# Two folded weight blocks come back from their exchange into other buffers

## The chip, the cores and the metric

The kernel runs on one core of a Trainium2 chip. The core has five engines that run side by side, each working through its own list of instructions in order: PE (TensorE, matrix products), DVE (VectorE), ACT (ScalarE), POOL (GpSimd) and SP (SyncE, which here only issues DMAs). ACT issues some DMAs too. The metric is the device time of one execution in microseconds (us); the time of a kernel is the median of its runs.

## The reference

Two attention branches A and B work on the same x (2048 rows of 448, in 16 heads of 28). Each branch has its own wqkv, w_phi and wo, and a gate mixes the two results:

```python
qkv = (x @ wqkv)                                  # per head q, k, v
pq = einsum("bhsd,hdf->bhsf", q, w_phi)           # the same w_phi for k
phi = concat([softmax(p), softmax(-p)], -1)       # for q and for k
kv = einsum("bhsf,bhsd->bhfd", phi_k, v);  z = sum_s phi_k
o = (phi_q @ kv) / (phi_q . z + 1e-6)
out = g * (o_A @ wo_A) + (1 - g) * (o_B @ wo_B)   # g = sigmoid(x . gate_w)
```

Since q is only ever used as q times w_phi, the kernel multiplies w_phi into the Q and K weights once ("the fold") and projects x with the folded weights. All is float32: each matrix is split into a high part (rounded for TensorE) and a low part (the rest), and products are summed over the parts.

## The kernel before, in words

The 2048 rows are cut into 16 tiles of 128, which are handled two at a time: eight steps u of branch A (loop from line 476), then eight steps of branch B (loop from line 580), then a tail whose order is a written list. A step of branch A or B has, on PE, a projection for K (`proj` with `wk`), one for V, one for Q where it is due, and `kv_acc`, which adds phi_k times V of the step before to the state. Around them: `k_shift` (DVE and POOL) takes the maximum off the K projection, `k_exp` (ACT) takes the exponentials, `k_sums` takes their sums (DVE, line 255), reciprocals (DVE, line 256) and products (POOL, line 264), and `kv_acc` (PE, line 289) waits for those products. `v_out` (ACT, line 272) copies a V projection out of PSUM. For Q: `q_front` (DVE, then DMAs `q_store` on SP and ACT to `qd` in DRAM), `q_load` (line 333, back from `qd` into `tq`), exponentials on ACT (341, 356), a POOL difference (349) and a DVE transposition (`q_turn`, 359); `num` (PE, 371) multiplies by the state. In branch B the A results are also finished: `a_turn` (DVE, 572), `n_rec` and `n_den`, `weights` (POOL, 403 and 404, with the gate), `n_mul` (POOL, 409).

Every engine works through its instructions in the order in which the program writes them, so a wait holds all that is written later for that engine. This holds for SP's DMAs too: a DMA whose source is not ready holds the ones behind it.

Branch B's folds go another way than A's. The strips of the weights are loaded (`load_strips`) and multiplied by w_phi on PE (`fold_strips`), and the products come out transposed. `turn_strips` turns 32x32 blocks on DVE (line 190), stores them to DRAM (`td`, four DMAs, line 192) and loads them back in the right layout (line 195 for three blocks of 128 rows, line 197 twice for the last 64 rows, which are held twice). `high_folded` (ACT, line 204) and `low_folded` (DVE, line 208) then make the high and the low part, each in one instruction of 128x1792. For K this begins in step u = 3 of branch A; the strips and the reloaded blocks lie in `wtb[1]`, the parts go to `wk[1]` (named wkb). For Q it begins in step u = 0 of branch B; strips and blocks lie in a tile named ctr, the parts go to `wq[1]` (named wka), which is first used by step u = 6 of branch B.

`wtb[0]` and `wtb[1]` are used for much else: the output weights come through them (`load_wo`, line 459; five of its seven loads are written in steps 4 and 5), and `q_turn` writes to them later. `wvr` holds the raw V weights: A's at the start, B's from step 0, read for the last time in step 3. `bd` and `wps` hold w_phi in two layouts; both have been read for the last time once the Q fold's products are through, and serve as output buffers in the tail.

Of the kernel before, what the change touches and what calls it, by code (L numbers as in the profile page):

```python
# [8 lines left out]
F32 = mybir.dt.float32  # L9
# [40 lines left out]
def hedgehog_mix(ctx: ExitStack, tc: tile.TileContext, xd, wv, wkt, wqt, wphi, wo, cmask, cpmask, out):  # L50
# [39 lines left out]
    make_identity(nc, ident)  # L90
    mask = raw.tile([PF, 4], F32, name="mask")
    wp = raw.tile([PF, 2, 4, HP], F32, name="wp")
    bd = wp_.tile([PF, 4, PF], F32, name="bd")
    wps = wp_.tile([P, D], F32, name="wps")
    wps = wps[:, :8 * HP].rearrange("p (b g m) -> p b g m", b=2, g=4)
    wk = [wp_.tile([P, 2, 4, D], F32R, name="wka"), wp_.tile([P, 2, 4, D], F32R, name="wkb")]
    wvs = [wp_.tile([P, 2, 4, DG], F32R, name="wva"), wp_.tile([P, 2, 4, D], F32R, name="wvb")]
    wq = [wp_.tile([P, 2, 4, D], F32R, name="wqa"), None]
# [23 lines left out]

    def load_wv(b, c, n=2, eng=nc.sync):
        w = (DG, D)[b]
        if c % 2 == 0:
            t = raw.tile([P, 2, w], F32, name=f"wvr{c}")
            for i in range(2):
                wvr[c + i] = t[:, i]
            if n == 2:
                return eng.dma_start(t, wv[c * P:(c + 2) * P, b * DG:b * DG + w].rearrange("(c p) n -> p c n", p=P))  # L130
        eng.dma_start(wvr[c], wv[c * P:(c + 1) * P, b * DG:b * DG + w])

    def high_w(wr, wh):
# [52 lines left out]
    def turn_strips(wt, ts, i):  # L186
        t = wt[:, :4 * D]
        o = t.rearrange("p (j i w m) -> p i w j m", i=2, w=2, m=HP)
        for j, ps in enumerate(ts):
            nc.vector.transpose(o[:, j], ps[:, :, :D].rearrange("p w (j m) -> p w j m", m=HP))  # L190
        for g in range(4):
            nc.sync.dma_start(td[i][:, g * P:g * P + P].rearrange("(j t) x -> t j x", t=HP),  # L192
                              t[HP * g:HP * g + HP].rearrange("t (j x) -> t j x", x=P))
        d = wt.rearrange("p (c x) -> p c x", c=4)
        nc.sync.dma_start(d[:, :3], td[i][:384].rearrange("(c p) x -> p c x", p=P))
        for p in (0, 64):
            nc.sync.dma_start(d[p:p + 64, 3], td[i][384:])

    def folded(wt, dst):
        return wt.rearrange("p (h m) -> p h m", m=HP)[:, :, :DH], [dst[:, i].rearrange("p c (h f) -> p (c h) f", f=DH) for i in range(2)]  # L200

    def high_folded(wt, dst):
        w, d = folded(wt, dst)
        nc.scalar.activation(d[0], w, AF.Copy)

    def low_folded(wt, dst, eng):
        w, d = folded(wt, dst)
        eng.tensor_tensor(d[1], w, d[0].bitcast(F32), OP.subtract)

    TERMS = [(c, 0, c) for c in range(3)] + [(4 + c, 0, c) for c in range(3)] + [(3, 0, 3)] + [(c, 1, c) for c in range(4)]  # L210

# [32 lines left out]
    def k_exp(k):  # L244
        for s in range(2):
            nc.scalar.activation(es[k][:, s], es[k][:, s], AF.Exp)  # L246
# [23 lines left out]
    def v_out(k, ps):  # L270
        v = vs[k % 2]
        nc.scalar.activation(v[:, :, :, :, :DH].rearrange("p w j q f -> p w (j q) f"), hb(ps[:, :, :D]), AF.Copy)  # L272
        if k < NU:
            nc.scalar.activation(glog[:, 2 * k:2 * k + 2], ps[:, :, D], AF.Copy)
# [65 lines left out]
    def q_exp0(k):  # L340
        nc.scalar.activation(eq[:, 0, :, :, :DH], tview(k), AF.Exp)
# [134 lines left out]
    for u in range(NU):  # L476

        if u in (2, 4):
            split_x(u // 2 + 1, 0, 4, 0)
        for c in WVS.get(u, ()):  # L480
            high_wv(1, c)
        if u == 5:
            nc.gpsimd.memset(eq[:, :, :, :, DH:], 0.0)
            for b in range(2):
                nc.gpsimd.memset(kvs[b], 0.0)
        if pq is not None:
            q_front(FRONTS[u - 1], pq)
            q_load(FRONTS[u - 1])
            pq = None
        pk = proj(u, wk[0], two_tile())  # L490
        if u > 1:
            k_sums(u - 1)
        if u in (2, 4):
            split_x(u // 2 + 1, 0, 4, 1)
        k_shift(u, pk)
        if u == 1:
            fold(wtqa, wq[0])
            k_sums(0)
        if u == 2:
            pq = proj(0, wq[0], two_tile())  # L500
            kv_acc(0)
        if u > 1:
            pv = proj(u, wvs[0], two_tile())
            v_out(u, pv)
        k_exp(u)

        if u == 0:
            wtqa = load_wt(wtb[0], wqt[0])
            load_x(2, 0, 4)
            for c in range(0, 4, 2):  # L510
                load_wv(1, c)
        if u == 1:
            load_strips(wtb[1], wkt[1])
            for r in range(4):
                nc.sync.dma_start(wps[HP * r:HP * r + DH], wphi[DH * r:DH * r + DH])
            nc.sync.dma_start(wos.rearrange("g (a f) n -> g a (f n)", f=DH),
                              wo.rearrange("(a g f) n -> g a (f n)", g=4, f=DH))
        if u in (2, 4):
            split_x(u // 2 + 1, 0, 4, 2)
        for c in WVS.get(u, ()):  # L520
            low_wv(1, c, nc.gpsimd)
        for c in WOS.get(u, ()):
            high_wo(c)
            low_wo(c)
        if u == 2:
            load_wo(0, 1)
            load_x(3, 0, 4)
        if u == 4:
            high_folded(wtb[1], wk[1])
            low_folded(wtb[1], wk[1], nc.vector)  # L530
            load_wo(4, 5, 2, 3)
        if u == 5:
            load_wo(6)
            start.close()
            mid = ctx.enter_context(tc.tile_pool(name="mid", bufs=1, side="right"))
            wtqb = load_strips(mid.tile([P, 2048], F32, name="ctr"), wqt[1])
        if u > 1:
            kv_acc(u - 1)
        if u == 3:
            turn_strips(wtb[1], fold_strips(1, wtb[1]), 0)  # L540
        if u == 7:
            pf = fold_strips(1, wtqb)
        if u == 5:
            pq = proj(FRONTS[u], wq[0], two_tile())
        if u == 6:
            q_exp0(0)
            q_min(0)
            q_exp1(0)
        if u == 7:
            q_turn(0)  # L550
# [29 lines left out]
    for u in range(NU):  # L580
# [5 lines left out]
        if n >= 0:  # L586
            a_turn(n)
            n_rec(n)
        q_exp0(m)
        q_min(m)  # L590
        if u == 0:
            turn_strips(wtqb, pf, 1)
# [11 lines left out]
        if u == 0:  # L604
            kv_acc(k - 1)
            state_copy(0)
            high_folded(wtqb, wq[1])
        else:
            k_sums(k - 1)
            if u == 1:  # L610
                n_mul(n)
        k_shift(k, pk)
        if u == 0:
            state_turn(0)
            q_turn(m)
            low_folded(wtqb, wq[1], nc.vector)
        pv = proj(u, wvs[1], two_tile())
        v_out(k, pv)
        k_exp(k)
        if u > 0:  # L620
            q_turn(m)
        if u == NU - 1:
            woh, wol = [wp_.tile([P, 7, D], F32R, name=n) for n in ("wkb", "wvb")]
            for w, d in ((woh, wod[0]), (wol, wod[1])):
                nc.sync.dma_start(w.bitcast(F32), d)
# [10 lines left out]

    obs = [wp_.tile([P, D], F32, name=n) for n in ("bd", "wps")]
    osb = wp_.tile([P, 2, 8, 8, DH], F32, name="wqa")  # L640
    qps, reads, maxs, mns, hls = {}, {}, {}, {}, {}
    A, B, C = (turn[0] + 2) % 3, turn[0], (turn[0] + 1) % 3
# [254 lines left out]
```

## Time and profile before

| | before |
|---|---|
| time, median of 3 runs | 361.88 us (359.70 to 362.72) |
| profiled execution, its own time | 361.31 us |
| profiled execution, span | 359.5 us |
| PE busy | 343.5 us (96%) |
| DVE busy | 275.1 us (77%) |
| POOL busy | 261.9 us (73%) |
| ACT busy | 121.4 us (34%) |
| mean granted clock of TensorE | 0.984 |

Times inside the profile are counted from the first instruction. Of the span, 1.8 us less than the execution's own time, almost all is PE work; what is left is where PE waits. Step u of branch A ends with its `kv_acc`: step 4's lies at 69 us in the profile for the products of step 3, step 5's at 87 us for those of step 4. Branch B begins at 115 us with a Q projection, its step 1 at 134 us, its step 2 at 150 us.

### The profile page before, as it was taken

What the parts mean: (1) busy time and instruction counts of PE and PEld (TensorE: products, weight loads), DVE (VectorE), ACT (ScalarE), POOL (GpSimd) and SP (SyncE); (2) the same over time, 40 slices, a digit from 0 to 9 for tenths busy, and PEclk for the clock granted to TensorE, in tenths of its full rate; (3) what the DMA queues carried; (4) which work ended last, traced back from release to release, by engine and by line L of the source; (5) the groups of instructions that cost most, each with busy time, mean ns of one, the idle gap of its engine ahead of it and who ended that gap; (6) DMA issues with size and microseconds to landing.
All of it is one profiled execution on the core that took longest, in us unless ns stands there. A gap on an engine that the chain in (4) does not pass through costs nothing.

```text
span 359.5 us, 8502 instructions
## 1 busy us (share of the span) xinstructions
PE 343.5 (96%) x3599; PEld 301.2 (84%) x3599; DVE 275.1 (77%) x315; ACT 121.4 (34%) x170; POOL 261.9 (73%) x228
## 2 busy tenths in 40 slices
PE   8999999983999979999999999999999999999995
PEld 7999888872988869898988989898888978888894
DVE  4328765526478779979989898899899999989740
ACT  4525335141244242133142231313223364434331
POOL 2453799745469423898988878886779999999850
PEclk9999999995899999999999999999999999999999
DMA  8796246751673761333313222349573472664111
GB/s 233 228 327 143 102 110 169 223 168 54 218 152 107 133 190 21 92 102 104 104 53 104 82 85 93 107 127 366 155 231 98 131 189 71 175 185 128 53 52 51
DMA packets 38958, 49.58 MB, mean 138 GB/s; under 512 B 11784, under 2 KB 32104, under 8 KB 38632
## 3 DMA queue, kind: packets, MB, share of 16 engines
q1 hardware_dynamic: 33768, 44.90, 42.5%
q10 hardware_dynamic: 5152, 4.13, 3.8%
q8 instruction: 28, 0.46, 0.6%
q14 instruction: 10, 0.08, 0.1%
HBM read 29.27 MB, written 21.36 MB: 141 GB/s over the span
## 4 chain that ended last, share of the span: by engine, by line
PE 72%; DMA 8%; POOL 7%; DVE 7%; ACT 2%; issue 1%; SPq 1%; POOLq 0%; ACTq 0%; DVEq 0%
PE two L225 45%; PE out L826 16%; PE two L371 4%; PE kv L289 3%; POOL e L264 3%; DMA wtb<-wos 2%; PE two L154 2%; DMA ctr<-td 2%; DMA wtb<-td 1%; DMA xrb<-in_xt 1%; DMA td<-wtb 1%; DVE sm L255 1%; POOL wva L409 1%; SPq L192 1%; PE kv L371 1%
## 5 line engine op out<-in xcount | busy, mean ns | idle before, releaser
L264 POOL TENSOR_TENSOR e<-e,rs 128x896 f32<-128x896 f32 x32 | 53.8, 1703 | 28.4 <-DVE rs L256 28.4
L225 PE MATMUL two<-wka,xg 128*128 128x448 f32 x352 | 73.8, 366 | 0.0
L225 PEld LDWEIGHTS two<-wka,xg 128*128 128x128 f32 x352 | 65.2, 188 | 6.3 <-issue 0.8
L272 ACT ACTIVATE vs<-two 128x896 f32<-128x896 f32 x16 | 14.7, 918 | 84.4 <-PE two L225 84.4
L225 PE MATMUL two<-wqa,xg 128*128 128x448 f32 x176 | 39.3, 380 | 2.1 <-ACT vs L272 2.1
L225 PEld LDWEIGHTS two<-wqa,xg 128*128 128x128 f32 x176 | 33.7, 195 | 6.5 <-ACT vs L272 2.6
L225 PE MATMUL two<-wva,xg 128*128 128x450 f32 x176 | 38.9, 372 | 0.2 <-ACT wva L134 0.2
L246 ACT ACTIVATE e<-e 128x896 f32<-128x896 f32 x32 | 28.7, 946 | 27.9 <-POOL e L242 27.8
L225 PE MATMUL two<-wvb,xg 128*128 128x448 f32 x176 | 37.2, 366 | 0.0
L359 DVE STREAM_TRANSPOSE wtb<-xrb 128x2048 f32<-128x2048 f32 x16 | 36.6, 2288 | 0.0
L225 PE MATMUL two<-wkb,xg 128*128 128x448 f32 x176 | 36.6, 363 | 0.0
L225 PEld LDWEIGHTS two<-wva,xg 128*128 128x128 f32 x176 | 33.1, 189 | 3.7 <-ACT wva L134 0.7
L255 DVE TENSOR_REDUCE sm<-e 128x32 f32<-128x896 f32 x32 | 33.0, 1072 | 4.2 <-ACT e L246 4.2
L242 POOL TENSOR_TENSOR e<-mx,e 128x896 f32<-128x896 f32 x16 | 27.2, 1703 | 11.6 <-DVE mx L241 11.5
L225 PEld LDWEIGHTS two<-wvb,xg 128*128 128x128 f32 x176 | 33.0, 188 | 2.8
L225 PEld LDWEIGHTS two<-wkb,xg 128*128 128x128 f32 x176 | 33.0, 188 | 2.3
L826 PE MATMUL out<-wkb,e 128*128 128x448 f32 x154 | 34.7, 370 | 0.1
L826 PEld LDWEIGHTS out<-wkb,e 128*128 128x128 f32 x154 | 28.6, 188 | 4.0 <-issue 0.8
L349 POOL TENSOR_TENSOR xrb<-qmn,tq 128x896 f32<-128x896 f32 x16 | 28.2, 1760 | 3.5 <-issue 3.1
L316 DVE TENSOR_REDUCE qmx<-two 128x32 f32<-128x896 f32 x14 | 15.0, 1073 | 16.0 <-PE two L225 16.0
L409 POOL TENSOR_TENSOR wva<-wva,cdd 128x896 f32<-128x896 f32 (+1 forms) x12 | 26.5, 2210 | 0.8
L409 POOL TENSOR_TENSOR ctr<-ctr,cdd 128x896 f32<-128x896 f32 (+1 forms) x12 | 26.6, 2213 | 0.6
(113 smaller groups left out, 579.9 us busy)
## 6 DMA issues: line engine op xcount, KB each, us to landing
tq<-qd SPq DMA_DIRECT2D x16, 448.0 KB
qd<-uq ACTq DMA_DIRECT2D x32, 112.0 KB
qd<-uq SPq DMA_DIRECT2D x32, 112.0 KB
od<-wva SPq DMA_DIRECT2D x8, 448.0 KB
wqa<-od SPq DMA_DIRECT2D x8, 448.0 KB
wod<-wtb SPq DMA_DIRECT2D x14, 224.0 KB
xrb<-in_xt SPq DMA_DIRECT2D x2, 1024.0 KB
out<-bd SPq DMA_DIRECT2D x8, 224.0 KB
```

The source lines that it names most:

```text
L225: nc.tensor.matmul(ps[:, i, :n], x[:, xc, o:o + P], w[:, k, wc], start=j == 0, stop=j == 10)
L242: nc.gpsimd.tensor_tensor(e5[:, 1], mx[:, 1, :, :, None].to_broadcast([P, 2, H, DH]), e5[:, 0], OP.subtract)
L246: nc.scalar.activation(es[k][:, s], es[k][:, s], AF.Exp)
L255: nc.vector.tensor_reduce(sm[:, s], e[:, s].rearrange("p (h f) -> p h f", f=DH), AX.X, OP.add)
L264: nc.gpsimd.tensor_tensor(e3, e3, rs[:, s, :, None].to_broadcast([P, HA, DH]), OP.mult)
L272: nc.scalar.activation(v[:, :, :, :, :DH].rearrange("p w j q f -> p w (j q) f"), hb(ps[:, :, :D]), AF.Copy)
L316: nc.vector.tensor_reduce(mx, p4, AX.X, OP.max)
L349: nc.gpsimd.tensor_tensor(eq[:, 1, :, :, :DH], mn.rearrange("p c a -> p a c")[:, :, :, None].to_broadcast([P, 8, 4, DH]), tview(k), OP.sub ...
L359: nc.vector.transpose(wtb[k % 2], eq.rearrange("p s a c f -> p (s a c f)"))
L371: nc.tensor.matmul(banks[r][32 * g:32 * g + 32, 256 * s:256 * s + 256], kvt[b][32 * r:32 * r + 32, s, g], eT[32 * r:32 * r + 32, s, g], st ...
L409: nc.gpsimd.tensor_tensor(c3, c3, dd.to_broadcast([P, 8, hi - lo, DH]), OP.mult)
L826: nc.tensor.matmul(outs[t % 2][:, :D], (hi, lo)[x][:, c], w[:, c], start=x == 0 and n == 0 and c == 0, stop=x == 1 and c == 6)
```

## The change

The blocks of the K fold come back into `wvr`, now one tile of 128x2048, instead of `wtb[1]`, in five DMAs instead of three: one per block of 128 rows, two for the last block. The high part is made by four ACT instructions of 128x448, written ahead of `k_exp` of step 4 and no longer behind it; the low part by four on DVE.

The blocks of the Q fold come back two at a time into `bd` and `wps`, which are made 512 wide. Their loads are written behind the V projection, `v_out` and `k_exp` of step u = 0 of branch B; they were written ahead of the Q store of that step. The high parts of the first two blocks follow there on ACT, their low parts on POOL; the other two blocks are loaded into the same two tiles when those have been read, their high parts are made by ACT in step 1 and their low parts by DVE in step 2.

```diff
-    bd = wp_.tile([PF, 4, PF], F32, name="bd")
-    wps = wp_.tile([P, D], F32, name="wps")
-    wps = wps[:, :8 * HP].rearrange("p (b g m) -> p b g m", b=2, g=4)
+    bd = wp_.tile([P, 512], F32, name="bd")[:PF, :4 * PF].rearrange("p (g c) -> p g c", g=4)
+    wps = wp_.tile([P, 512], F32, name="wps")[:, :8 * HP].rearrange("p (b g m) -> p b g m", b=2, g=4)
+    wvrs = raw.tile([P, 2048], F32, name="wvr")
...
     def load_wv(b, c, n=2, eng=nc.sync):
         w = (DG, D)[b]
-        if c % 2 == 0:
-            t = raw.tile([P, 2, w], F32, name=f"wvr{c}")
-            for i in range(2):
-                wvr[c + i] = t[:, i]
-            if n == 2:
-                return eng.dma_start(t, wv[c * P:(c + 2) * P, b * DG:b * DG + w].rearrange("(c p) n -> p c n", p=P))
+        t = wvrs[:, c // 2 * 2 * DG:][:, :2 * w].rearrange("p (c n) -> p c n", c=2)
+        wvr[c] = t[:, c % 2]
+        if n == 2:
+            wvr[c + 1] = t[:, 1]
+            return eng.dma_start(t, wv[c * P:(c + 2) * P, b * DG:b * DG + w].rearrange("(c p) n -> p c n", p=P))
...
-        d = wt.rearrange("p (c x) -> p c x", c=4)
-        nc.sync.dma_start(d[:, :3], td[i][:384].rearrange("(c p) x -> p c x", p=P))
-        for p in (0, 64):
-            nc.sync.dma_start(d[p:p + 64, 3], td[i][384:])
...
+    def load_folded(i, bufs, cs):
+        for c in cs:
+            for p in (0, 64)[:1 + (c == 3)]:
+                n = P if c < 3 else 64
+                nc.sync.dma_start(bufs[c][p:p + n], td[i][c * P:c * P + n])
+
+    def high_folded(bufs, dst, cs):
+        for c in cs:
+            nc.scalar.activation(dst[:, 0, c].rearrange("p (h f) -> p h f", f=DH),
+                                 bufs[c].rearrange("p (h m) -> p h m", m=HP)[:, :, :DH], AF.Copy)
+
+    def low_folded(bufs, dst, cs, eng):
+        for c in cs:
+            h, l = [dst[:, i, c].rearrange("p (h f) -> p h f", f=DH) for i in range(2)]
+            eng.tensor_tensor(l, bufs[c].rearrange("p (h m) -> p h m", m=HP)[:, :, :DH], h.bitcast(F32), OP.subtract)
...
+        if u == 4:
+            high_folded(fk, wk[1], range(4))
         k_exp(u)
...
         if u == 4:
-            high_folded(wtb[1], wk[1])
-            low_folded(wtb[1], wk[1], nc.vector)
+            low_folded(fk, wk[1], range(4), nc.vector)
             load_wo(4, 5, 2, 3)
...
             turn_strips(wtb[1], fold_strips(1, wtb[1]), 0)
+            fk = [wvrs[:, 512 * c:512 * c + 512] for c in range(4)]
+            load_folded(0, fk, range(4))
...
         q_exp0(m)
+        if u == 1:
+            high_folded(fq, wq[1], (2, 3))
         q_min(m)
...
             state_copy(0)
-            high_folded(wtqb, wq[1])
...
             q_turn(m)
-            low_folded(wtqb, wq[1], nc.vector)
         pv = proj(u, wvs[1], two_tile())
         v_out(k, pv)
         k_exp(k)
-        if u > 0:
+        if u == 0:
+            fq = [wp_.tile([P, 512], F32, name=n) for n in ("bd", "wps")] * 2
+            for cs in ((0, 1), (2, 3)):
+                load_folded(1, fq, cs)
+                if cs[0] == 0:
+                    high_folded(fq, wq[1], cs)
+                    low_folded(fq, wq[1], cs, nc.gpsimd)
+        else:
             q_turn(m)
+        if u == 2:
+            low_folded(fq, wq[1], (2, 3), nc.vector)
```

What this does to the order of the instructions shows at three places. The first is ACT around the K fold, steps 4 and 5 of branch A; before it reads (272 is `v_out`, 246 is `k_exp`, 204 is `high_folded`):

```order
L272 ACTIVATE vs_150<-two_748 128x32x28
L274 ACTIVATE glog<-two_748 128x2
L246 ACTIVATE e<-e 128x896 x2
L204 ACTIVATE wkb<-wtb_124 128x1792
L272 ACTIVATE vs_151<-two_853 128x32x28
L274 ACTIVATE glog<-two_853 128x2
```

and now, with `high_folded` in line 202:

```order
L272 ACTIVATE vs_151<-two_747 128x32x28
L274 ACTIVATE glog<-two_747 128x2
L202 ACTIVATE wkb<-wvr 128x448 x4
L246 ACTIVATE e<-e 128x896 x2
L272 ACTIVATE vs_152<-two_858 128x32x28
L274 ACTIVATE glog<-two_858 128x2
```

The one large copy has become four, and they have moved past the exponentials of step 4. The second place is SP's queue around the Q fold, before (192 stores to `td`, 195 and 197 load it back, 325 and 333 are the Q store and load, 566 and 568 take the gate through DRAM):

```order
L192 DMA td_88<-ctr 32x14x128 x4
L195 DMA ctr<-td_88 128x3x512
L197 DMA ctr<-td_88 64x512 x2
L325 DMA qd_92<-uq_129 32x4x224 x2
L333 DMA tq_131<-qd_92 128x896
L566 DMA gd<-glog 32x4x16 x4
L568 DMA gate<-gd 128x64
L325 DMA qd_93<-uq_130 32x4x224 x2
L333 DMA tq_132<-qd_93 128x896
```

and now (the loads are in line 198, the gate in 569 and 571):

```order
L191 DMA td_88<-ctr 32x14x128 x4
L325 DMA qd_92<-uq_129 32x4x224 x2
L333 DMA tq_131<-qd_92 128x896
L198 DMA bd<-td_88 128x512
L198 DMA wps<-td_88 128x512
L198 DMA bd<-td_88 128x512
L198 DMA wps<-td_88 64x512 x2
L569 DMA gd<-glog 32x4x16 x4
L571 DMA gate<-gd 128x64
L325 DMA qd_93<-uq_130 32x4x224 x2
L333 DMA tq_132<-qd_93 128x896
```

The Q store and load now stand ahead of the reloads of the fold, and the second pair of reloads, which waits until `bd` and `wps` have been read, stands ahead of the gate. The third place is ACT around the Q fold, before (294 copies the state, 562 is the gate's exponential):

```order
L294 ACTIVATE kvs_75<-kv 128x8x28
L204 ACTIVATE wka<-ctr 128x1792
L272 ACTIVATE vs_150<-two_1312 128x32x28
L246 ACTIVATE e<-e 128x896 x2
L562 ACTIVATE glog<-glog 128x16
L341 ACTIVATE xrb<-tq_131 128x32x28
L356 ACTIVATE xrb<-xrb 128x32x28
```

and now (the gate's exponential is in line 565):

```order
L294 ACTIVATE kvs_75<-kv 128x8x28
L272 ACTIVATE vs_151<-two_1312 128x32x28
L246 ACTIVATE e<-e 128x896 x2
L202 ACTIVATE wka<-bd 128x448
L202 ACTIVATE wka<-wps 128x448
L565 ACTIVATE glog<-glog 128x16
L341 ACTIVATE xrb<-tq_131 128x32x28
L202 ACTIVATE wka<-bd 128x448
L202 ACTIVATE wka<-wps 128x448
L356 ACTIVATE xrb<-xrb 128x32x28
```

`v_out` and `k_exp` of branch B's first step now come ahead of the fold's high parts, and the gate's exponential stands behind the first two of them.

More of the change, by code (lines that the diff above doesn't have):

```diff
@@ L193, in turn_strips @@
                               t[HP * g:HP * g + HP].rearrange("t (j x) -> t j x", x=P))
-        d = wt.rearrange("p (c x) -> p c x", c=4)
-        nc.sync.dma_start(d[:, :3], td[i][:384].rearrange("(c p) x -> p c x", p=P))
-        for p in (0, 64):
[L197 to L208, printed above, removed]
+    def load_folded(i, bufs, cs):
[11 more added lines that the diff above has]
+            eng.tensor_tensor(l, bufs[c].rearrange("p (h m) -> p h m", m=HP)[:, :, :DH], h.bitcast(F32), OP.subtract)
     TERMS = [(c, 0, c) for c in range(3)] + [(4 + c, 0, c) for c in range(3)] + [(3, 0, 3)] + [(c, 1, c) for c in range(4)]
@@ L635, in hedgehog_mix @@
             kv_acc(k - 1)
-    obs = [wp_.tile([P, D], F32, name=n) for n in ("bd", "wps")]
+    obs = [wp_.tile([P, 512], F32, name=n)[:, :D] for n in ("bd", "wps")]
     osb = wp_.tile([P, 2, 8, 8, DH], F32, name="wqa")
```

## The prediction

> **What bounds the kernel now.** I read the page's summary first: the busy time of PE, and its slices of busy time and granted clock.
>
> ```profile
> PE 343.5 (96%) x3599; PEld 301.2 (84%) x3599; DVE 275.1 (77%) x315; ACT 121.4 (34%) x170; POOL 261.9 (73%) x228
> PE   8999999983999979999999999999999999999995
> PEclk9999999995899999999999999999999999999999
> ```
>
> PE is busy nearly everywhere. A slice is 9 us, and two places show a dent: the ninth and tenth slices (near 80 us), where the clock falls too, and the fifteenth (near 130 us). These are the two folds of branch B. Next the chain of waits around the first dent, in order of time (start, duration, what):
>
> ```profile
> 66.77 4.16 DMA td<-wtb
> ...
> 70.97 0.38 SPq L195
> ...
> 71.45 0.51 SPq L197
> ...
> 72.05 4.96 DMA wtb<-td
> ...
> 77.12 1.71 ACT wkb L204
> ...
> 78.86 2.03 DVE wkb L208
> 80.88 2.00 DVE sm L255 x2
> ...
> 82.90 0.56 DVE rs L256
> ...
> 83.60 3.36 POOL e L264 x2
> ...
> 87.01 1.72 PE kv L289 x64
> ```
>
> The K fold goes out to DRAM and comes back at 77.0; ACT makes the whole high part, DVE the whole low part, and only then does DVE come to the sums of step 4, which PE needs through POOL. The timeline shows what PE loses, and that the exponentials had long been done:
>
> ```profile
> 71.70 1.79 ACT L246 ACTIVATE e<-e 128x896 f32<-128x896 f32 x2 [1.35 <-POOL e L242]
> 74.64 4.68 PE L225 MATMUL two<-wva,xg 128*128 128x450 f32 x22
> 87.01 1.72 PE L289 MATMUL kv<-e,vs 128*29 128x56 f32 x64 [7.68 <-POOL e L264]
> 88.66 6.16 PE L225 MATMUL two<-wqa,xg 128*128 128x448 f32 x22
> ```
>
> PE stands 7.68 us. The projection after it takes 6.16 us, against 4.68 in the row above, since the clock has fallen. The windows of one us (PE busy, then four engines, granted clock, DMA share, GB/s) say when:
>
> ```profile
> 75.00:76.00 1.00, 0.94 (x4) 1.00 1.03 279
> 76.00:77.00 1.00, 0.03 (x1) 1.00 0.31 82
> ...
> 81.00:82.00 1.00, 0.00 (x0) 0.00 (x0) 1.00 (x2) 0.00 (x0) 0.00 (x0) 0.75 0.03 8
> 91.00:92.00 1.00, 1.00 (x5) 0.88 (x5) 0.00 (x0) 1.00 (x3) 1.00 (x1) 0.63 0.21 77
> ```
>
> (The first two are of POOL alone: busy, clock, DMA share, GB/s.) The clock halves at about 81.5, 2.2 us after PE went idle at 79.3, and is whole again at about 91.7, so 4.7 us of work run at half speed and cost 2.35 us. Last, the timeline around the second dent:
>
> ```profile
> 121.53 1.16 DVE L318 TENSOR_TENSOR uq<-two,qmx 128x448 f32<-128x448 f32 x2
> 125.61 4.74 PE L225 MATMUL two<-wvb,xg 128*128 128x448 f32 x22
> 126.01 1.05 SPq L325 DMA_DIRECT2D qd<-uq  x2
> 131.41 1.70 ACT L204 ACTIVATE wka<-ctr 128x1792 fp32r<-128x1792 f32 x1 [5.30 <-DMA ctr<-td]
> 131.96 0.34 SPq L333 DMA_DIRECT2D tq<-qd  x1
> 133.01 0.90 ACT L272 ACTIVATE vs<-two 128x896 f32<-128x896 f32 x1
> 133.96 4.76 PE L225 MATMUL two<-wqa,xg 128*128 128x448 f32 x22 [2.08 <-ACT vs L272]
> 135.49 0.20 ACT L562 ACTIVATE glog<-glog 128x16 f32<-128x16 f32 x1
> 136.26 1.73 SPq L566 DMA_DIRECT2D gd<-glog  x4
> 140.70 0.34 SPq L568 DMA_DIRECT2D gate<-gd  x1
> ```
>
> ACT waits for the Q fold until 131.4, with `v_out` behind it; PE needs that copy and stands 2.08 us. The fold itself is not due until step 6. After this PE hardly waits, but POOL is close behind it:
>
> ```profile
> 139.09 0.35 POOL L388 TENSOR_TENSOR cdd<-wva,crs 128x64 f32<-128x64 f32 x1 [8.75 <-DVE crs L383]
> 142.74 0.27 POOL L403 TENSOR_TENSOR cden<-cden,gate 128x32 f32<-128x32 f32 x1 [0.89 <-DMA gate<-gd]
> 145.05 3.36 POOL L264 TENSOR_TENSOR e<-e,rs 128x896 f32<-128x896 f32 x2 [1.64 <-DVE rs L256]
> 161.61 3.36 POOL L264 TENSOR_TENSOR e<-e,rs 128x896 f32<-128x896 f32 x2
> 165.02 0.84 PEld L289 LDWEIGHTS kv<-e,vs 128*29 128x29 f32 x64 [0.58 <-POOL e L264]
> ```
>
> From 145.05 POOL works without a gap until its products of 161.61, and PE's state update at 165.02 waits 0.58 us for them. So what PE wins at 132 counts only as far as POOL's 145.05 moves too.
>
> **The change, part by part.** The profiled execution took 361.31 us with a span of 359.5; I sum against 361.31, which is 0.57 below the median of the three runs (361.88) and well inside their range of 3 us.
>
> *K's reload.* The stores to `td` and the start of the reload at 70.97 stay. `wvr` was read for the last time in step 3, so the target costs no wait. Five DMAs take the place of three: with 0.48 us from one issue to the next in the rows above, the last goes out at about 73.0 and no longer at 72.05. I let it land at 77.1 all the same: the DMA engines were full (share 1.03) until 76, so bytes and not issues set the end. Were it the issue, it would be 78.0; were it the last byte, 76.3.
>
> [...] The row of the four stores to `td`, which land 4.16 us after the last of them was issued, is of overlapped DMAs, and I keep the overlap.
>
> *K's high and low parts.* I need the price of one block of 128x448 on ACT and on POOL:
>
> ```profile
> 106.61 0.56 ACT L134 ACTIVATE wtb<-wtb 128x448 fp32r<-128x448 f32 x1
> 107.24 1.16 POOL L137 TENSOR_TENSOR wtb<-wtb 128x448 fp32r<-128x448 f32 x1 [2.37 <-ACT wtb L134]
> ```
>
> Three blocks are done while the fourth lands. The last costs ACT 0.56; DVE's last low part (a quarter of 2.03, some 0.55) runs beside the exponentials. These now come behind: `k_exp` waits for the fold and ends at 77.2 + 0.56 + 1.79 = 79.5 and no longer at 73.5. That costs `v_out` of step 5 nothing, since PE ends its V projection at 79.3. DVE's first sum needs only the first half, done at 78.65. So from the landing to the sums: 0.1 + 0.56 + 0.9 = 1.6 us and no longer 80.88 - 77.01 = 3.9. The second half is ready at 79.5, before the first sum ends (78.7 + 1.0). The rest of the chain (2.00, 0.56, 3.36) is unchanged. Gain 3.9 - 1.6 - 0.1 for the landing = **2.2 us**; with the other landings 1.3 and 3.0. PE still stands some 5.5 us, and the clock falls as before, so I leave those 2.35 us in.
>
> *Output weights.* SP no longer waits for `low_folded` with the loads of blocks 2 and 3; they come earlier, behind the reload in the same queue. Nothing waited for them before, nor will now: no gain.
>
> *Q's ACT wait.* `v_out` no longer stands behind the fold: it starts when PE's V projection is through (130.4) and ends at 131.3; the stall of **2.08 us** goes. `k_exp`, with its 1.79 us, ends at 133.1. What is late next is POOL's 145.05, which hangs on two things. One is DVE, which in order must first do the gate's arithmetic after ACT's exponential, then `a_turn`, the Q work and the sums. ACT's exponential comes behind two high parts: 133.1 + 2 x 0.56 = 134.3 against 135.49, if the first two blocks have landed by 133. I expect that: SP's Q store, whose data DVE has ready at 122.7, goes out 3.2 us earlier than 126.01, without the fold's megabyte ahead of it. A pair like this is seen later:
>
> ```profile
> 142.36 0.79 SPq L325 DMA_DIRECT2D qd<-uq  x2
> 145.54 0.34 SPq L333 DMA_DIRECT2D tq<-qd  x1
> ```
>
> With 3.2 us from store to load, and a us more since the `td` stores are still moving, the Q load goes out at 127, the two blocks behind it at 127.5 and 128, and they land by 132 even with 4 us each. So DVE comes 1.2 us earlier.
>
> *Q's low parts and the gate.* POOL makes two low parts, 2 x 1.16 us, from 133.8 to 136.1, in its idle 8.75 us: free. But SP's second pair of loads waits for each of them, and behind it stand the gate's DMAs, the Q store of step 1 and its load. SP issues the second pair at 134.9 and 136.1 to 137.2 (three issues, 0.48 apart), then the gate's four stores at 137.3 against 136.26. With 4.4 us to the gate's load (136.26 to 140.70) and 2.0 more until POOL starts (142.74), POOL's line 403 starts at 143.7, 1.0 late. POOL then needs 0.7 us to its products: 144.5 against 145.05. DVE would have allowed 143.9. So POOL gains 0.55; I take **0.4**, since the ACT queue's Q store now falls on the gate's load. The bounds are 1.2 (the gate not late) and a loss of 3.8 (worked out in the last rival).
>
> *Q's other parts.* The second pair's high parts, 1.1 us, stand on ACT ahead of the exponential of line 356, which waits for POOL anyway; their low parts cost DVE 1.1 us in step 2, where it has lost the 2.03 of line 208 for good. I cost both at nothing; uncovered it would be 1.1 us. The wider tiles and the single V tile move no instruction.
>
> Sum: 361.31 - 2.2 - 0.4 = **358.7 us**. From 165 on PE is the bound and both terms reach the end.
>
> **The rivals.** *The clock does not fall.* PE's idle stretch shrinks from 7.7 to 5.5 us. If that no longer halves the clock, the 2.35 us go too: 358.7 - 2.35 = 356.4. Against it: here the clock fell 2.2 us into the idle time. [...] Chance 0.10.
>
> *The gate is not late.* The low parts or the loads go faster, and DVE alone decides: 361.31 - 2.2 - 1.2 = 357.9. For it: there is 1 us only between the two. Chance 0.14.
>
> *The split brings nothing for K.* Five smaller DMAs end by their issues or later (78.0 to 78.6), and the gain falls to about 1: 361.31 - 1.0 - 0.4 = 359.9. For it: the reload's last 128 KB took 4.96 us from issue to landing before. Against: the full engines. [...] Chance 0.16.
>
> *SP's new waits decide, and it gets slower.* If the first two blocks land as late as before's fold did after its last issue (4.96 us), behind a Q load that still goes out at 131.96, they land at 137.5. ACT's high parts end at 138.7, POOL's low parts at 140.5, SP's gate stores go out at 141.7, the gate lands 6.4 us later, and POOL's products start at 148.9 and no longer at 145.05: a loss of 3.8 and, with K's gain, 361.31 + 3.8 - 2.2 = 362.9. It decides from a landing at about 136 on (a loss of 2.2). For it: two waits in a row on one queue. Against: 4 us between that and the landing that I expect. Chance 0.08.
>
> **How the numbers follow.** The forecast has what is left, 0.52, with 358.7 and its own range 357.7 to 359.9: K's landing 1 us either way, less the extremes. The runs before spread over 3 us, so a median may lie 1 us off. The range leaves out most of the last rival and half of the first: 356.5 to 361.2. A measurement of this kernel tells about 1% from no change; 1% below 361.88 is 358.3, above it 365.5. Below 358.3: most of the first two rivals and a quarter of the forecast, 0.36. Above 365.5: a part of the last rival and a little for what I do not see, 0.05. Within: 0.59.
>
> **What would show it.** Right: line 202's last copy of K ends at 77.7 or so, DVE's sums of step 4 start 2 us earlier and PE's stall near 80 us is about 5.5; the stall of 2.08 is gone, DVE has no large line 208, and POOL's line 403 waits for the gate longer than 0.89. Wrong: K's last block lands after 78; the second `v_out` is held by `k_exp`; ACT's line 202 waits for `bd` in branch B; or PE waits for POOL at 149 and 165 for longer than it won.

## The result and the profile after

| | before | changed |
|---|---|---|
| time, median of 20 runs each, taken in turn | 361.81 us | 359.46 us |
| ratio to before, 95% interval | | 0.9946 (0.9921 to 0.9972) |
| change by the ratio | | 2.0 us less (1.0 to 2.9) |
| profiled execution, its own time | 361.31 us | 363.02 us |
| a second profiled execution | | 359.51 us |

The change makes the kernel 2.0 us faster by the ratio of the runs and 2.35 by the two medians: within 1%, as forecast (358.7 us, 2.6 less than the profiled execution). A second and a third group of runs of the same kernel gave 359.27 and 359.30 us. (Executions over 1.5% above the fastest of their kernel, among them one of 419.1 us at a granted clock of 0.755, are left out of the ratios and of the medians from here on.)

The first profiled execution of the changed kernel took 363.02 us; only 4 of its 20 runs lie at 362 to 364. The timeline shows what was different in it: SP's stores of the K fold to `td`, and PE's stall behind them.

```profile
67.24 4.02 SPq L191 DMA_DIRECT2D td<-wtb  x4
...
88.48 1.72 PE L289 MATMUL kv<-e,vs 128*29 128x56 f32 x64 [9.37 <-POOL e L264]
```

In the second execution these stores went out at 63.67, with nothing changed in the program. In both the fold needs about the same time from its stores to the state update, 21.2 and 20.9 us; in the first it began 3.6 us late. The delay can be followed back along SP's queue to four small loads of w_phi, which SP issues in step 1 of branch A. First execution, then second:

```profile
25.57 7.71 SPq L517 DMA_DIRECT2D wps<-in_wphi  x4
```

```profile
25.72 1.73 SPq L517 DMA_DIRECT2D wps<-in_wphi  x4
```

In the first they waited 6.3 us for earlier loads to land. The copy of the output weights behind them went out at 33.55 and not at 28.34, the load that waits for that copy at 51.46 (in the profile of before, with the copy at 29.76, at 47.52), and what stands behind that in SP's queue came later too. So I read the change from the second execution, whose 359.51 us lies at the median, and quote from it below. First its page, which answers to the three lines that the prediction starts from:

```profile
PE 345.2 (97%) x3599; PEld 301.9 (84%) x3599; DVE 277.0 (77%) x319; ACT 122.5 (34%) x176; POOL 264.7 (74%) x230
PE   8999999985999999999999999999999999999995
PEclk9999999996999999999999999999999999999998
```

The dent near 80 us is smaller, and the one near 130 us is gone. Next the chain of waits around the K fold (start, duration, what):

```profile
66.46 3.95 DMA td<-wtb
...
70.43 0.34 SPq L198
...
72.18 0.51 SPq L198
...
72.73 4.12 DMA wvr<-td
...
77.42 0.94 ACT e L246
...
78.39 0.87 DVE sm L255
...
81.20 3.36 POOL e L264 x2
...
84.61 1.72 PE kv L289 x64
```

The fold lands at 76.9, as before (77.0), and the update of PE comes 7.75 us later (84.61 - 76.86) and no longer 10.0 (87.01 - 77.01): 2.25 us less. The reload itself, from its first issue, takes 6.4 us (76.86 - 70.43) against 6.0 (77.01 - 70.97), so from there to the update it is 14.2 us against 16.0: 1.9 less. The other 0.5 us by which the update comes earlier are those by which the reload went out earlier; the program does not explain them, and over the twelve traces read here the stores of the fold take 6.4 to 7.5 us until the reload can go out. DVE's 2.03 us and most of ACT's 1.71 are gone from the chain. The timeline shows the blocks one by one:

```profile
73.00 0.58 ACT L202 ACTIVATE wkb<-wvr 128x448 fp32r<-128x448 f32 x1 [2.81 <-DMA wvr<-td]
...
76.94 0.58 ACT L202 ACTIVATE wkb<-wvr 128x448 fp32r<-128x448 f32 x1 [0.77 <-DMA wvr<-td]
...
77.55 0.63 DVE L208 TENSOR_TENSOR wkb<-wvr,wkb 128x448 fp32r<-128x448 f32 x1 [0.72 <-ACT wkb L202]
...
84.61 1.72 PE L289 MATMUL kv<-e,vs 128*29 128x56 f32 x64 [5.44 <-POOL e L264]
86.26 6.11 PE L225 MATMUL two<-wqa,xg 128*128 128x448 f32 x22
```

ACT copies the first block at 73.0 and the last at 76.94, DVE's last low part takes 0.63 us beside the exponentials, and PE stands 5.44 us. The clock falls as before, at about 82.4, to 0.50, and is whole again at about 89.3 (PE busy, PE's loads, DVE, ACT, POOL, granted clock, DMA share, GB/s):

```profile
82.00:83.00 1.00, 0.00 (x0) 0.00 (x0) 0.96 (x2) 0.00 (x0) 1.00 (x2) 0.72 0.27 99
...
89.00:90.00 1.00, 1.00 (x6) 0.91 (x5) 0.00 (x0) 0.91 (x2) 1.00 (x2) 0.86 0.61 226
```

Then the place of the Q fold, in the timeline of branch B's step 0:

```profile
129.50 4.75 PE L225 MATMUL two<-wqa,xg 128*128 128x448 f32 x22
...
131.24 1.16 POOL L208 TENSOR_TENSOR wka<-bd,wka 128x448 fp32r<-128x448 f32 x1 [3.22 <-ACT wka L202]
...
134.71 2.71 SPq L569 DMA_DIRECT2D gd<-glog  x4
...
140.52 0.27 POOL L403 TENSOR_TENSOR cden<-cden,gate 128x32 f32<-128x32 f32 x1 [2.20 <-DMA gate<-gd]
...
141.51 3.36 POOL L264 TENSOR_TENSOR e<-e,rs 128x896 f32<-128x896 f32 x2 [0.32 <-DVE rs L256]
```

PE's stall of 2.08 us is gone, and POOL makes its low parts in idle time. So far all is as forecast. What was not forecast lies in step 2, 30 us later, on DVE and POOL:

```profile
162.88 0.69 DVE L208 TENSOR_TENSOR wka<-bd,wka 128x448 fp32r<-128x448 f32 x1
...
163.04 2.52 POOL L413 TENSOR_TENSOR wva<-ctr 128x896 f32<-128x896 f32 x1
...
163.49 2.55 DVE L208 TENSOR_TENSOR wka<-wps,wka 128x448 fp32r<-128x448 f32 x1
...
169.00 0.35 POOL L388 TENSOR_TENSOR cdd<-wva,crs 128x64 f32<-128x64 f32 x1 [3.44 <-DVE crs L383]
...
179.08 0.99 PE L289 MATMUL kv<-e,vs 128*29 128x56 f32 x64 [0.58 <-POOL e L264]
```

The two low parts of Q's third and fourth block take DVE 0.69 and 2.55 us, where one takes 0.63 at 77.55. POOL then waits 3.44 us for DVE, and PE for POOL.

How much each stage won or lost is read from the starts of the state updates (line 289), counted from the last update of branch A (the one whose start is 124.69 in the profile of before and 122.37 here), in us:

| profiled execution | last of A | 2nd of B | 3rd of B | last of B |
|---|---|---|---|---|
| before | 0 | 40.34 | 56.25 | 129.65 |
| changed | 0 | 39.11 | 56.71 | 130.11 |
| K's part alone | 0 | 40.04 | 55.93 | 129.35 |
| Q's part alone | 0 | 39.31 | 56.90 | 130.34 |
| low parts on POOL | 0 | 39.09 | 55.00 | 128.40 |
| low parts on DVE, two instructions later | 0 | 39.11 | 55.00 | 128.42 |

(The last two are experiments, below.) Branch A ends 2.3 us earlier: the 1.9 us of K and the earlier reload. The Q part wins 1.23 us up to the second update of branch B and loses 1.69 us to the third: 0.46 worse than before, and it stays so to the end. This is not the scatter of one trace: the last column is 130.1 to 130.4 in all six traces with Q's part as it is in the change, and 129.35 and 129.65 in the two without it.

### The profile page after: what moved, and what is told of

It reads as the page before. It is cut to its first block, busy times and chain, and to the rows that moved or that the text cites. A ratio compares the mean times of both kernels' runs of the same rounds, so it can differ in the third digit from the quotient of the medians.

```text
span 361.2 us, 8516 instructions
## 1 busy us (share of the span) xinstructions
PE 344.7 (95%) x3599; PEld 301.1 (83%) x3599; DVE 276.0 (76%) x319; ACT 122.4 (34%) x176; POOL 264.8 (73%) x230
## 4 chain that ended last, share of the span: by engine, by line
PE 73%; DVE 11%; POOL 6%; DMA 4%; issue 2%; ACT 2%; SPq 1%; POOLq 0%; DVEq 0%; ACTq 0%
PE two L225 44%; PE out L838 16%; PE kv L289 4%; PE two L371 4%; POOL e L264 3%; PE two L153 2%; DVE sm L255 2%; PE two L434 2%; POOL wva L409 2%; DMA wvr<-td 1%; DMA td<-wtb 1%; DVE wva L575 1%; DVE wtb L359 1%; DVE wka L208 1%; PE kv L371 1%
## 5 line engine op out<-in xcount | busy, mean ns | idle before, releaser
L289 PEld LDWEIGHTS kv<-e,vs 128*29 128x29 f32 x1024 | 14.1, 111 | 16.2 <-POOL e L264 12.4
```

The source lines that it names most:

```text
L289: nc.tensor.matmul(kvp[b][32 * r:32 * r + DH + 1, g], v[:, w, h // 2, h % 2], phi[:, :, hs:hs + DH], start=(u == 0 and w == 0 and g == 0), ...
```

## The experiments

**The two parts apart.** First only K's part: the reload of Q, its high and its low part are the old code (shown are the lines that come back; the new ones for Q go out).

```diff
         if u == 0:
             turn_strips(wtqb, pf, 1)
+            load_q_old(1, wtqb)
...
             state_copy(0)
+            high_old(wtqb, wq[1])
...
             q_turn(m)
+            low_old(wtqb, wq[1], nc.vector)
```

> Only the K fold is changed as in the change; the Q fold comes back into its old buffer at its old place. My theory: the K part brings 2.2 us (1.3 to 3.0), so 0.994 of the kernel before, and from the landing of the last K block to PE's state update pass 8 us or a little less, where it was 10.0; the stall of 2.1 us near 132 us stays. Rival (the split brings nothing for K, the whole gain is Q's stall): within 0.5 us of the kernel before.

Then only Q's part, with the old code for K:

```diff
-        if u == 4:
-            high_folded(fk, wk[1], range(4))
         k_exp(u)
...
-            low_folded(fk, wk[1], range(4), nc.vector)
+            high_old(wtb[1], wk[1])
+            low_old(wtb[1], wk[1], nc.vector)
...
-            fk = [wvrs[:, 512 * c:512 * c + 512] for c in range(4)]
-            load_folded(0, fk, range(4))
+            load_q_old(0, wtb[1])
```

> Only the Q fold is changed; the K fold comes back into its old buffer, with one copy behind the exponentials. My theory: PE's stall near 132 us goes, but POOL moves by 0.4 us only, since the gate lands later, so 0.4 us (0 to 1.2) faster, 0.999 of the kernel before. Rival (the gain is Q's stall): about 2 us faster, 0.9945. If DVE's low part of the last block, which took 2.56 us in the changed kernel's profile beside a POOL instruction, costs PE time, the gain is smaller by up to 0.5 us.

Measured (median, ratio to before, its 95% interval): K alone 359.29 us (0.9942, 0.9913 to 0.9971), Q alone 361.54 us (0.9985, 0.9962 to 1.0007); before, in the same group, 361.56. In the trace of K alone the update comes 8.3 us after the landing (87.08 - 78.81; 8 or a little less was expected), and the stall near 132 us stays (1.77). All of the gain that can be told from nothing is K's; Q's part is worth between 0.3 us of loss and 1.4 of gain by its runs, and by the table of the traces 0.7 us of loss (130.34 against 129.65). The two do not quite agree.

**The changed kernel once more**, for a second profile, and later a third time beside other kernels:

> The changed kernel once more, to have it beside the others on one chip and a second profile of it: 0.9946 of the kernel before, within 0.25%. The profile on record was of an execution of 363 us, in which the K fold went out to DRAM 3.6 us later than in the profile before; if that is chance, it goes out at about 63.7 us here and PE's stall is 5.5 us.

> The changed kernel once more, beside the others on the same chip: 359.3 us by all theories, 2.0 to 2.5 us below the kernel before.

Measured: 359.27 us (0.995, 0.9926 to 0.9973) and 359.30 us (0.9928, 0.9902 to 0.9954).

**K: what the single blocks bring.** One DMA for the first three blocks, as before; the four ACT and DVE pieces stay.

```diff
-            load_folded(0, fk, range(4))
+            nc.sync.dma_start(wvrs.rearrange("p (c x) -> p c x", c=4)[:, :3],
+                              td[0][:384].rearrange("(c p) x -> p c x", p=P))
+            load_folded(0, fk, (3,))
```

> The changed kernel with the first three K blocks reloaded by one DMA, as before the change; the four pieces of the high and the low part stay. My theory (the bytes set the landing; three blocks are worked on while the fourth lands): the last landing stays, but three copies and the last come one after the other behind two landings that lie closer together, so up to 1 us slower than the changed kernel, more likely 0 to 0.5. Rival (the smaller DMAs cost time): 0.5 to 1 us faster than the changed kernel.

Measured: 360.25 us (0.9972, 0.9949 to 0.9995). The chain of waits, from the reload to the update:

```profile
70.11 5.31 DMA wvr<-td
...
75.44 0.59 ACT wkb L202
...
84.51 1.72 PE kv L289 x64
```

All blocks are there at 75.4, ACT copies them back to back, and the update comes 9.1 us after the landing (84.51 - 75.42), against 7.75 in the changed kernel and 10.0 before. So the pieces without the landing block by block gain 0.9 us there, and the landing block by block 1.3 more. In this execution the reload was quick, 5.3 us from its first issue to the landing (75.42 - 70.11), so that from issue to update it takes 14.4 us, only 0.2 more than the changed kernel's 14.2. Whether it is quicker in general can be judged from the profiled executions of this study: with five DMAs the reload took 5.4 to 6.9 us in nine, with three 5.3, 6.0 and 7.5 in three. That is one spread, and the 5.3 us are its low end; with the 6.4 of the changed kernel the update would come 1.1 us later here, and 1.3 later than in the changed kernel. The runs have it 1.0 us above the changed kernel, with intervals that overlap: they point the same way but do not prove it. The rival, 0.5 to 1 us faster than the changed kernel (at most 0.9932 of before), lies outside the interval and falls.

Next the order on ACT: the exponentials of step 4 ahead of the four copies again.

```diff
-        if u == 4:
-            high_folded(fk, wk[1], range(4))
         k_exp(u)
+        if u == 4:
+            high_folded(fk, wk[1], range(4))
```

> The changed kernel with the exponentials of step 4 ahead of the high parts of K again. By my sum, from the landing of the last block to the sums pass 0.1 + 0.56 + 0.55 (the last low part) and no longer 0.1 + 0.56 + 0.9: about 0.3 us earlier, but then both sums come after them as before, so equal within 0.5 us: the gain is that of the pieces. Rival (the move past the exponentials is what counts): the gain of K goes, some 2 us slower than the changed kernel.

Measured: 358.9 us (0.9944, 0.9919 to 0.997), no difference that can be told from the changed kernel. In its trace the last copy starts at 76.78 and the update at 84.15, 7.4 us later and no longer 7.7: in the traces, putting the copies ahead of the exponentials gains nothing and costs 0.3 us, as expected. The rival, a loss of 2 us, falls.

**Q: the low parts in step 2.** The trace points to the two DVE instructions. In the first experiment POOL makes them, in steps 3 and 4:

```diff
-        if u == 2:
-            low_folded(fq, wq[1], (2, 3), nc.vector)
+        if u in (3, 4):
+            low_folded(fq, wq[1], (u - 1,), nc.gpsimd)
```

> The changed kernel with the low parts of Q's last two blocks taken from DVE in step 2 of branch B and given to POOL, one in step 3 and one in step 4. My theory, from the traces of the changed kernel and of the run with Q alone: DVE's second low part takes 2.56 us and not 0.63, because it stands still beside a POOL instruction of 2.5 us, and from the state update of 165 us to the next PE takes 17.6 us where it took 15.9; without it the 1.7 us come back (15.9 between the two updates), so 1.7 us faster than the changed kernel, 0.990 of the kernel before. Rival (PE waits there for what the earlier stall left over, whatever DVE does): the 17.6 us stay.

Measured: 357.78 us (0.9909, 0.9872 to 0.9945), 1.5 us below the changed kernel, and once more:

> The kernel with the low parts of Q's third and fourth block on POOL in steps 3 and 4 once more, beside the others on the same chip: 357.8 us by its first run, 1.5 us below the changed kernel, if that difference is real; within 0.5 us of the changed kernel if it was the scatter of the runs.

Measured: 357.31 us (0.9886, 0.9858 to 0.9915), 2.0 us below the changed kernel of the same group. In the trace of the first, POOL's line 413 takes 2.13 us and no longer 2.52, and POOL waits 0.70 us for DVE and no longer 3.44:

```profile
161.65 2.13 POOL L413 TENSOR_TENSOR wva<-ctr 128x896 f32<-128x896 f32 x1
164.48 0.35 POOL L388 TENSOR_TENSOR cdd<-wva,crs 128x64 f32<-128x64 f32 x1 [0.70 <-DVE crs L383]
```

This does not yet say whether DVE loses by having the work or by doing it beside POOL's line 413. So DVE keeps the two low parts, but does them two instructions later, behind its transpositions of line 575, where POOL is idle:

```diff
             a_turn(n)
+            if u == 3:
+                low_folded(fq, wq[1], (2, 3), nc.vector)
             n_rec(n)
...
-        if u == 2:
-            low_folded(fq, wq[1], (2, 3), nc.vector)
```

> The same two low parts of Q stay on DVE, but stand behind the two transpositions of A's result (line 575) and no longer ahead of them; nothing else differs from the changed kernel. In the trace of the kernel with the two low parts on POOL, POOL is through with line 413 at 163.78 and DVE with its transpositions at 163.82, so at this place POOL stands idle. Theory: in the changed kernel DVE's low part stands still because POOL's line 413 is running (2.55 us where it takes 0.63 alone), and POOL's line 413 stands still for the rest of the first one (2.52 where it takes 2.13). Then here both low parts take about 0.63 us each, line 413 takes 2.13 again, POOL's line 388 comes 1.3 us later than in the kernel with the low parts on POOL and no longer 3.1 us later, the slack of about 1.4 us before the products takes that up, and the time is that of the kernel with the low parts on POOL: 357.8 to 358.3, 1.0 to 1.5 us below the changed kernel's 359.3. Rival: what costs is that DVE has this work at all in this stage, or its reads are slow whatever POOL does. Then the second low part takes 2 us or more here too and the time stays at 359 to 359.5.

Measured: 358.1 us (0.9901, 0.987 to 0.9931), 1.2 us below the changed kernel of the same group, as expected; the 0.8 us that it lies above the kernel with the low parts on POOL, beside it, are within the intervals. The timeline of DVE and POOL there:

```profile
163.90 2.34 DVE L575 STREAM_TRANSPOSE wva<-two 128x1024 f32<-128x1024 f32 x2
166.16 0.58 DVE L208 TENSOR_TENSOR wka<-bd,wka 128x448 fp32r<-128x448 f32 x1
166.66 0.61 DVE L208 TENSOR_TENSOR wka<-wps,wka 128x448 fp32r<-128x448 f32 x1
```

```profile
164.06 2.13 POOL L413 TENSOR_TENSOR wva<-ctr 128x896 f32<-128x896 f32 x1
167.82 0.36 POOL L388 TENSOR_TENSOR cdd<-wva,crs 128x64 f32<-128x64 f32 x1 [1.63 <-DVE crs L383]
```

POOL's line 413 ends at 166.19, as DVE's first low part begins, and all three have their short durations again: 0.58, 0.61, 2.13. In the table of stages this kernel stands like the one with the low parts on POOL (55.00 and 128.42 against 55.00 and 128.40). The rival, that the work itself costs, falls: in the traces the same work costs 1.7 us at one place and nothing two instructions later. There Q's part as a whole is worth 1.2 us (128.42 against the 129.65 of before).

**The clock.** Is the clock kept up if PE has something to do in its stall? 24 transpositions of a unit matrix, into a part of PSUM that nothing reads, stand ahead of the wait of step 5:

```diff
             load_wo(6)
+            for _ in range(24):
+                nc.tensor.transpose(kvb[:, 1, 256:384], ident, ident)
             start.close()
```

> The changed kernel with 24 transpositions of the identity matrix on PE between step 5's V projection and the state update that waits for the K fold; their result goes to an unused part of PSUM and is not read. If the fall of the clock in this stall costs what I read from the trace (2.35 us at half speed), the clock stays at 1.0 and the kernel is about 2 us faster than the changed one (near 357.4 us). Rival: the clock falls anyway, or PE's stall was not what counts behind it: no difference. The transpositions take some 4.6 us and end before the 5.5 us of the stall.

Measured: 358.19 us (0.9882, 0.9841 to 0.9923), but not for the reason expected. The timeline of PE:

```profile
78.74 2.78 PE L536 MATMUL kv<-ident 128*128 128x128 f32 x24
83.81 0.99 PE L289 MATMUL kv<-e,vs 128*29 128x56 f32 x64 [2.28 <-POOL e L264]
84.73 6.29 PE L225 MATMUL two<-wqa,xg 128*128 128x448 f32 x22
```

They took 2.78 us, 2.28 stayed idle, and the clock fell all the same, only later: the update ran at full clock (0.99 us), the projection behind it at half (6.29). Its median lies 1.1 us below the changed kernel's, which was not run in this group. In its trace branch A ends 1.2 us earlier (121.18 against 122.37): the update starts 0.8 us earlier, mostly because the reload went out 0.6 earlier (69.83), and from it to the next one pass 16.1 us and no longer 16.6; only this half microsecond can be the clock. So the last one has 40 of them, on top of the low parts on POOL:

> The kernel with the low parts on POOL and 40 transpositions on PE in the wait for the K fold (24 took 2.8 us and not the 4.6 that I had expected, and left an idle 2.3 us, enough for the clock to fall). 40 take 4.6 us and leave under 1 us of the stall: the clock stays at 1.0, which brings about 2 us over the kernel with the low parts on POOL alone. Rival (the clock falls by PE's work per window, and transpositions do not count as work): no difference, and half speed after the stall as before.

```profile
78.78 4.53 PE L536 MATMUL kv<-ident 128*128 128x128 f32 x40
84.65 0.99 PE L289 MATMUL kv<-e,vs 128*29 128x56 f32 x64 [1.34 <-POOL e L264]
85.58 4.76 PE L225 MATMUL two<-wqa,xg 128*128 128x448 f32 x22
```

The window behind the update has the clock (third number from the end) whole:

```profile
86.00:87.00 1.00, 1.00 (x7) 0.92 (x6) 0.00 (x0) 0.71 (x1) 0.26 (x1) 1.00 0.01 2
```

Measured: 355.56 us (0.9845, 0.9813 to 0.9877). Update and projection take 0.99 and 4.76 us. In the two traces of the kernel without them they take 1.72 and 5.49, and 1.72 and 6.23: 1.5 and 2.2 us more. That is about what separates the time from the 357.78 and 357.31 us of that kernel (2.2 and 1.8); all six runs with the 40 lie below all twelve without. The rival, that transpositions do not count as work for the clock, falls. This is the best version: 5.9 us below the kernel before and 3.7 below the changed one of the same group, by the medians.

## Why the prediction was right, and where it was wrong

**K's part: right, in size and mechanism.** Forecast 2.3 us from the landing on and 0.1 back for a later landing; measured 2.25 and, counted from the first issue of the reload, 0.4 back, which is 1.9 where I had 2.2. Over the nine profiled executions with five DMAs it is 14.0 us on average from issue to update (13.4 to 14.6), 2.0 less than the 16.0 of before. The stall of 5.5 us was 5.44. Whether bytes set the landing, as I chose, is not shown: it came 6.4 us after the first issue, where I had 6.1 and would have had 7.0 by the issues, and in the first profiled execution, where the last block landed at 80.33, the DMA engines were busy to 1.01 from 77 to 78, to 0.83 in the next microsecond and to 0.47 in the one behind it. The rival that the split brings nothing (landing at 78.0 to 78.6, which is 7.0 to 7.6 after the first issue) fell.

**The clock: right for the traces, closer than I thought.** It fell in the shorter stall as well, so the first rival fell there. But I had argued from one delay, 2.2 us into the idle time. Over the traces the fall came 2.0 to 4.9 us into it, so a stall of 5.5 us leaves little room. And of 43 runs of the changed kernel ten have a mean granted clock of 0.995, at 357.8 to 359.2 us, and the others at most 0.990; 68 runs of the kernel before have 0.989 at most. By these means (an estimate: 0.005 x 357.7 x 2) such a run has some 3.6 us at half clock in all, while the trace read here has 6.8 in this stall alone. So in some runs a part of that rival's gain may be there; no trace of such a run was kept.

**Q's stall and the gate: mechanism right, size wrong.** The step that put POOL's products 0.4 us earlier was mis-sized: the table has 1.23 us up to the second update, and POOL's products of 145.05 come 1.22 us earlier, counted from the last update of A (141.51 - 122.37 = 19.14, against 145.05 - 124.69 = 20.36). I had let the gate hold them, 1.0 us late. Its four stores do go out later, by 0.8 us (134.71 - 122.37 = 12.34 against 136.26 - 124.69 = 11.57), but POOL's line 403 starts only 0.1 us later (18.15 against 18.05). I had carried the delay on unchanged through the 4.4 us from the stores to the load and the 2.0 to POOL; both came out shorter, 4.0 and 1.8 us. So what happened is the rival "the gate is not late", with DVE deciding (1.2 us). The rival in which SP's new waits decide fell: the first blocks had landed before ACT came to them.

**Q's other parts: wrong, and this is the step that failed.** I had costed the second pair's low parts at nothing in step 2, "where it has lost the 2.03 of line 208 for good", and at 1.1 us uncovered. They cost 1.69 us on the path. There are two errors in that step. The 2.03 us were saved in step 0; in step 2 DVE had nothing to give, since POOL's line 388 waits there for the transpositions that stand behind the low parts, with 0.70 us of wait even without them. And I took the duration from a place where POOL is idle (busy to 0.00 from 78 to 83 in the profile of before). The rows of step 2 read as if the two engines stood still for each other: POOL's line 413 starts at 163.04, while DVE's first low part still runs (162.88 to 163.57), and takes 0.4 us more than its 2.13; DVE's second one starts at 163.49, ends at 166.04, and so has 0.48 us left behind the end of line 413 at 165.56. For the same form DVE took 2.55 us there and 0.63 at 77.55, and the experiment that moves the low parts by two instructions, where they take 0.58 and 0.61, shows that the place decides. I had not asked what POOL would be doing beside them.

That the forecast came out is in part luck, since its errors nearly cancel: 0.8 us of gain too little for the gate, 1.7 too much for the low parts, 0.3 too much for K, and 0.5 that the sum did not have, for the reload that went out earlier. From 2.6 us of gain that leaves 2.6 + 0.8 - 1.7 - 0.3 + 0.5 = 1.9; the traces show 361.31 - 359.51 = 1.8, the runs 2.0 by the ratio. My chances were thus placed on the wrong cases: the forecast's own working (gate late, low parts free) was right in neither of its Q terms.

**What stays open.** Why the runs give Q's part alone 0.5 us of gain by the ratio and its trace 0.7 of loss; whether the landing block by block is worth the 1.3 us that the chain suggests or the 1.0 of the runs, or less; and why the small loads of w_phi hold SP's queue for 7.71 us in one execution and for 3.67 and 1.73 in two others.

## What to carry to other kernels

Work that is moved to an engine with idle time has to be priced at the place where it will run: who waits there for that engine, and what runs beside it there. For an instruction of DVE, look for the one of POOL that will run beside it; here two instructions' distance decided 1.7 us in the traces (a low part of 2.55 us beside POOL's line 413, of 0.61 behind it) and 1.2 in the runs. A stall of PE that can't be removed can still be filled with work that is thrown away, if that keeps the clock: 40 small transpositions were worth 2 us here (2.2 and 1.8 by the medians).

## What the runs showed of the hardware that was not expected

*Some instructions of DVE and POOL took longer beside each other.* Beyond the rows above (2.55 us against 0.63 on DVE, 2.52 against 2.13 on POOL), one of DVE with a single input took longer too: a small step of the gate's arithmetic, beside POOL's low part that runs from 131.24 to 132.40, ends just behind it, at 132.42. Its reciprocal, which follows beside POOL's second low part (132.35 to 133.50), takes its usual 0.25:

```profile
131.75 0.67 DVE L566 TENSOR_SCALAR glog<-glog 128x16 f32<-128x16 f32 x1 [3.39 <-ACT glog L565]
132.46 0.25 DVE L567 RECIPROCAL glog<-glog 128x16 f32<-128x16 f32 x1
```

In the profile of before the same two instructions have POOL idle beside them:

```profile
135.72 0.17 DVE L563 TENSOR_SCALAR glog<-glog 128x16 f32<-128x16 f32 x1 [0.56 <-ACT glog L562]
135.93 0.25 DVE L564 RECIPROCAL glog<-glog 128x16 f32<-128x16 f32 x1
```

The step takes 0.66 or 0.67 us in eight traces with POOL's low part beside it and 0.17 in the two without. Why the step took longer and the reciprocal did not, no row here shows.

*The clock fell after the idle time.* In the experiment with 24 transpositions PE was idle for 2.28 us, from about 81.5, and resumed at 83.81; the windows of one us (columns as above) show the clock whole until then and at half behind it, from about 84.9 to 88.3:

```profile
83.00:84.00 1.00, 0.20 (x16) 0.20 (x20) 0.44 (x1) 0.00 (x0) 1.00 (x2) 1.00 0.27 90
84.00:85.00 1.00, 1.00 (x65) 0.92 (x55) 0.00 (x0) 0.00 (x0) 1.00 (x1) 0.94 0.31 102
85.00:86.00 1.00, 1.00 (x4) 0.87 (x4) 0.00 (x0) 0.56 (x1) 0.41 (x1) 0.50 0.06 23
...
88.00:89.00 1.00, 1.00 (x5) 0.91 (x5) 0.00 (x0) 1.00 (x3) 1.00 (x2) 0.85 0.44 161
```

With 1.34 us idle, behind 40 transpositions, it did not fall. Whether there is a limit between the two was not tried, nor whether the length alone decides. The half clock lasts 3.4 us here, 6.8 in the trace of the changed kernel (82.4 to 89.3) and 10.2 in that of before (81.5 to 91.7): one, two and three times about 3.4 us. In the seven other traces read here in which it falls in this stall, it lasts 3.4 us once, 6.8 four times and 10.2 twice.

*Two more DMAs for the same megabyte cost nothing that stands out of the spread:* 5.4 to 6.9 us from the first issue to the last landing with five, 5.3 to 7.5 with three.
